# Attention and a squared-ReLU feed-forward on one core: all loads plain on one queue, weights cast on three engines, the whole kernel as one scheduled list

## The chip, the cores and the metric

One core of one Trainium2 chip. The metric is device time in microseconds (us), the median of several executions. The engines are PE (matmuls), ACT (ScalarE), DVE (VectorE), POOL (GpSimd) and SP, which here only issues DMAs.

## The reference

Causal attention in a window of 64 keys over 8 batches, 8 heads, 576 tokens, head size 64; then a feed-forward over the 4608 tokens: 512 to 2048, squared ReLU, 2048 to 512. All inputs and the output are fp32.

```python
scores = (q @ k.transpose(0, 1, 3, 2)) / sqrt(64)
scores = where((rel >= 0) & (rel < 64), scores, -1e9)      # rel = query - key
x = softmax(scores) @ v                                     # -> 4608 x 512
h = maximum(x @ w_in, 0.0)
out = (h * h) @ w_out
```

## The kernel before

Work goes in chunks of 128 tokens and groups of four chunks (512 tokens, 9 groups). For each chunk: k and q are cast to fp16 and transposed; scores (S), exp on ACT, mask on DVE, values (V) on PE, normalising on DVE, transpose of x (X). For each group: 16 up-projection steps (ReLU on ACT, square on DVE), 16 out-projection steps of four matmuls, four evictions. Groups 0 and 1 do their up-projection chunk by chunk, so that PE has work while data still arrives. Groups 0 to 2 of q and k are loaded as one DMA each, with four tokens in a partition (runs of 1 KB); later groups and all of v come in chunks (runs of 256 B).

The parts that the argument needs (cut):

```python
    def load_w_in(quar):                       # casts fp32 -> fp16 on its way, on POOL's queue
        nc.gpsimd.dma_start(
            out=w_in_q[quar][:],
            in_=moe_w_in[:, quar * FQ:(quar + 1) * FQ].rearrange("(c p) n -> p c n", p=P))

    def behind(w, n):                          # makes the SP queue wait until w has landed
        nc.sync.dma_start(out=gate16[:, n:n + 1], in_=w[0:1, 0, 0:1])

    def load_kq(src, g):                       # one group; pieces end where a batch of 576 tokens ends
        st = kqst.tile([P, H, 4 * D], FP32, name="kq_st", tag="kq_st")
        p = 0
        while p < P:
            b, t0 = divmod(512 * g + 4 * p, 64 * NB)
            n = min(P - p, (64 * NB - t0) // 4)
            nc.sync.dma_start(out=st[p:p + n],
                in_=src[b, :, t0:t0 + 4 * n, :].rearrange("h (t r) d -> t h (r d)", r=4))
            p += n
        return st
    # ...
    load_w_in(2)
    cast_v(3, vst[3])
    behind(w_in_q[1], 0)
    kst[1], qst[1] = load_kq(k, 1), load_kq(q, 1)
    # ...
    for g in range(2, NTB + 1):                # the steady part: steps sorted by a place in the group
        # ...
        if g + 2 < NTB:
            steps += [(0.03 + 0.17 * j, load_chunk, 4 * g + 8 + j) for j in range(4)]
            if g + 2 >= KQ_XBAR:
                steps.append((0.8, transposes_xbar, g + 2))    # k and q transposed by DMA
        run(steps)
```

Group 0 fills all 128 partitions from one batch. Group 1 straddles two batches, so its load is two pieces, of 16 and 112 partitions; group 2's has 32 and 96.

The softmax here doesn't subtract the row's maximum and nothing guards it: scores larger than these inputs give would overflow.

## Time and profile before

| | before |
|---|---|
| median time | 330.55 us (329.89 to 330.83; the first three runs) |
| profiled span | 328.0 us |
| third q group (q2) landed | 65.50 us |
| first full-width up-projection (u2.0, group 2) | 90.76 us |
| last matmul | 323.86 us |

Landing times, and the rates in GB/s further down, are counted from the trace's semaphore and packet records. Rates are of bytes read; the page's own GB/s row counts bytes moved to the destination, so a casting load shows half of what it reads.

The page of the kernel before. A digit is the busy share of a fortieth of the span, in tenths; PEclk is the granted clock of PE.

```profile
span 328.0 us, 7256 instructions
...
PE 306.0 (93%) x2896; PEld 162.2 (49%) x2896; DVE 189.7 (58%) x431; ACT 158.7 (48%) x273; POOL 109.6 (33%) x181
...
PE   7758899989899999999999999999999999999994
...
PEclk9999999999999999999999999999999999999998
DMA  7999999989693969598949995799589022000111
```

PE is full from a quarter of the span on, and loose before. DMA is full where PE is loose.

What PE waited for, longest first (total us, times, longest), kernel before:

```profile
PE sc L223 <- DMA qT<-q: 3.7, 5, 0.8
PE hps L298 <- DVE xT L265: 3.7, 3, 2.1
PE run_ps L193 <- DVE k L120: 1.4, 4, 0.5
PE run_ps L193 <- ACT q L120: 1.4, 2, 1.1
```

The first line is in the steady part: five groups start their scores 0.75 us before the DMA transpose of q has ended. Busy time by stretches shows it as PE's missing 0.77 us (start:end length, PE, PEld, DVE, ACT, POOL, clock, DMA share, GB/s):

```profile
120.00:140.00 20.00, 19.23 (x165) 8.96 (x165) 12.17 (x26) 10.62 (x19) 6.21 (x10) 1.00 0.91 177
140.00:160.00 20.00, 19.22 (x146) 9.06 (x147) 10.75 (x24) 9.46 (x17) 6.05 (x10) 1.00 0.92 206
```

In the first part, the timeline of POOL shows casts of k and q that begin as their loads land. The bracket is the idle time before, and what ended it:

```profile
28.62 1.17 POOL L120 CAST k<-kq_st 128x512 f16<-128x512 f32 x2 [7.86 <-DMA kq_st<-in_k_dram]
...
33.62 1.17 POOL L120 CAST q<-kq_st 128x512 f16<-128x512 f32 x2 [3.14 <-DMA kq_st<-in_q_dram]
...
61.17 1.17 POOL L120 CAST k<-kq_st 128x512 f16<-128x512 f32 x2 [15.01 <-DMA kq_st<-in_k_dram]
65.64 1.17 POOL L120 CAST q<-kq_st 128x512 f16<-128x512 f32 x2 [3.31 <-DMA kq_st<-in_q_dram]
```

### The profile page before, as it was taken

To read this page: it belongs to the slowest core of one execution; us is meant where nothing else is said; L and a number is where in the kernel's file an instruction comes from. 1 tells how busy PE (TensorE), PEld (TensorE's weight loads), DVE (VectorE), ACT (ScalarE), POOL (GpSimd) and SP (SyncE) were. 2 spreads that over 40 slices of the span, in tenths; PEclk is the share of its full clock that TensorE was granted. 3 is DMA by queue.
4 is the path that set the end of the run, shared out by engine and by line. 5 is a ranking of instruction groups with operands and counts; after the bars stand their busy time and mean duration, and the time that the engine had idled before them with its cause. 6 is when DMAs were issued, how large, how long until landed. Compare 5 with 4: busy or idle time off the path is not lost.

```text
span 328.0 us, 7256 instructions
## 1 busy us (share of the span) xinstructions
PE 306.0 (93%) x2896; PEld 162.2 (49%) x2896; DVE 189.7 (58%) x431; ACT 158.7 (48%) x273; POOL 109.6 (33%) x181
## 2 busy tenths in 40 slices
PE   7758899989899999999999999999999999999994
PEld 3347668874445444444444444444444444444442
DVE  3776888677656656654656466646654675334400
ACT  3634665485246545544554365445644563444411
POOL 1742850199834522433345243614360000000000
PEclk9999999999999999999999999999999999999998
DMA  7999999989693969598949995799589022000111
GB/s 239 211 179 244 161 165 202 206 188 202 154 219 87 225 140 234 109 215 176 229 114 199 192 228 119 169 224 225 115 165 204 34 66 60 36 34 32 64 64 65
DMA packets 136741, 50.79 MB, mean 155 GB/s; under 512 B 121860, under 2 KB 132100, under 8 KB 136708
## 3 DMA queue, kind: packets, MB, share of 16 engines
q1 hardware_dynamic: 132484, 46.15, 65.6%
q0 software_dynamic: 4224, 4.19, 8.2%
q8 instruction: 22, 0.36, 0.5%
q14 instruction: 11, 0.09, 0.1%
HBM read 36.70 MB, written 9.44 MB: 141 GB/s over the span
## 4 chain that ended last, share of the span: by engine, by line
PE 60%; DMA 13%; DVE 10%; SPq 6%; ACT 5%; issue 3%; POOL 2%; ACTq 0%; POOLq 0%
PE ops L315 28%; PE hps L286 20%; DMA qT<-q 7%; PE hps L298 5%; PE sc L223 3%; SPq L201 3%; ACT hrelu L279 3%; DVE h L280 3%; PE av L247 3%; DMA kq_st<-in_q_dram 2%; DMA st<-in_v_dram 2%; DVE x_sb L252 2%; SPq L84 2%; DVE pm L236 2%; DMA st<-in_q_dram 1%
## 5 line engine op out<-in xcount | busy, mean ns | idle before, releaser
L280 DVE SCALAR_TENSOR_TENSOR h<-hps,hrelu 128x512 f16<-128x512 f32 x144 | 99.3, 690 | 102.4 <-ACT hrelu L279 101.4
L315 PE MATMUL ops<-w_out,h 128*128 128x512 f16 x576 | 145.3, 380 | 0.0
L279 ACT ACTIVATE hrelu<-hps 128x512 f32<-128x512 f32 x144 | 86.1, 598 | 102.7 <-PE hps L286 81.7
L286 PE MATMUL hps<-xT,w_in 128*128 128x512 f16 x448 | 115.1, 379 | 0.0
L315 PEld LDWEIGHTS <-h 128*128 128x128 f16 x576 | 53.7, 98 | 60.9
L286 PEld LDWEIGHTS <-w_in 128*128 128x128 f16 x448 | 42.8, 98 | 50.2
L232 ACT ACTIVATE pm<-sc 128x512 f16<-128x512 f32 x72 | 39.0, 596 | 22.0 <-PE sc L223 21.4
L114 POOL CAST k<-st 128x512 f16<-128x512 f32 x24 | 14.8, 615 | 74.2 <-DMA st<-in_k_dram 73.4
L298 PE MATMUL hps<-xT,w_in 128*128 128x128 f16 x512 | 32.2, 219 | 4.6 <-DVE xT L265 3.7
L321 ACT ACTIVATE osb<-ops 128x512 f32<-128x512 f32 x36 | 21.5, 598 | 28.5 <-PE ops L315 28.5
L298 PEld LDWEIGHTS <-w_in 128*128 128x128 f16 x512 | 29.6, 98 | 6.5 <-issue 5.6
L252 DVE TENSOR_TENSOR x_sb<-av,rden 128x256 f16<-128x256 f32 x72 | 30.6, 425 | 2.5
L236 DVE TENSOR_TENSOR pm<-pm,mask_inner 128x512 f16<-128x512 f16 x56 | 26.9, 505 | 4.1 <-ACT pm L232 3.5
L126 POOL CAST v_ev<-st 128x512 f16<-128x512 f32 x36 | 23.2, 644 | 10.7 <-DMA st<-in_v_dram 8.0
L127 POOL COPY v_od<-v_ev 64x512 f16<-64x512 f16 x36 | 22.4, 623 | 2.3
L129 POOL COPY v_od<-v_ev 64x512 f16<-64x512 f16 x35 | 22.2, 633 | 2.0
L247 PEld LDWEIGHTS <-pm 128*64 128x64 f16 x576 | 12.3, 110 | 14.2 <-issue 11.4
L114 POOL CAST q<-st 128x512 f16<-128x512 f32 x24 | 15.6, 651 | 8.9 <-DMA st<-in_q_dram 8.9
L247 PE MATMUL av<-v_od,pm 128*64 128x65 f16 x288 | 16.3, 197 | 0.5 <-DVE pm L236 0.5
L247 PE MATMUL av<-v_ev,pm 128*64 128x65 f16 x288 | 16.3, 197 | 0.0
L223 PE MATMUL sc<-qT,kT 64*128 64x64 f16 x504 | 15.0, 191 | 1.4 <-DVE x_sb L252 1.1
L223 PEld LDWEIGHTS <-kT 64*128 64x128 f16 x504 | 10.7, 95 | 4.9 <-issue 1.9
(57 smaller groups left out, 121.2 us busy)
## 6 DMA issues: line engine op xcount, KB each, us to landing
out_dram<-osb SPq DMA_DIRECT2D x36, 256.0 KB, 2.6
st<-in_v_dram SPq DMA_DIRECT2D x32, 256.0 KB, 5.3
st<-in_k_dram SPq DMA_DIRECT2D x21, 256.0 KB, 4.1
st<-in_q_dram SPq DMA_DIRECT2D x21, 256.0 KB, 5.1
w_in<-in_moe_w_in_dram POOLq DMA_DIRECT2D x4, 512.0 KB, 6.3
w_out<-in_moe_w_out_dram POOLq DMA_DIRECT2D x4, 512.0 KB, 8.6
kq_st<-in_k_dram SPq DMA_DIRECT2D x1, 1024.0 KB
kq_st<-in_q_dram SPq DMA_DIRECT2D x1, 1024.0 KB, 8.1
```

The source lines that it names most:

```text
L114: copy(out=kq16(key, i // 4)[:, :, i % 4, :].rearrange("p a (b d) -> p a b d", d=D), in_=st[:].rearrange("p (a b) d -> p a b d", b=2))
L126: nc.gpsimd.tensor_copy(out=v_ev[:, :, 0:D], in_=st[:])
L223: nc.tensor.matmul(sc[hh][:, hp, blk, :], keys, qTs["q", g][r0:r0 + 64, hp, a + 64 * blk:a + 64 * blk + 64], start=True, stop=True)
L232: nc.scalar.activation(out=pm[:], in_=sc[hh][:], func=AF.Exp, scale=1.0 / float(D) ** 0.5)
L236: nc.vector.tensor_tensor(out=pm[:], in0=pm[:], in1=mask, op=ALU.min)
L247: nc.tensor.matmul(av[64 * blk:64 * blk + 64, h % 4, 0:65], pms[i][h % 2][:, h // 2, blk, :], vv[:, h, 0:65], start=True, stop=True)
L252: nc.vector.tensor_tensor(out=x_sb[:, 2 * half:2 * half + 2, i % 2, :].rearrange("p c (b d) -> p c b d", d=D), in0=av[:, :, 0:D].rearrange ...
L279: nc.scalar.activation(out=hrelu, in_=hps, func=AF.Relu, scale=H_SCALE)
L280: nc.vector.scalar_tensor_tensor(out=out, in0=hps, scalar=0.0, in1=hrelu, op0=ALU.max, op1=ALU.mult)
L286: nc.tensor.matmul(hps[:], w_in_q[f // 4][:, c, f % 4 * P:(f % 4 + 1) * P], xT_of(g)[:, :, c, :], start=(c == 0), stop=(c == DMC - 1))
L298: nc.tensor.matmul(hps[:, f, :], w_in_q[fq][:, c, f * P:(f + 1) * P], xT_of(g)[:, i % 4 // 2, c, a:a + P], start=(c == 0), stop=(c == DMC ...
L315: nc.tensor.matmul(hold[ts % 2][:], h2s["h", g][:, 4 * fq + f, ts * P:(ts + 1) * P], w_out_q[fq][:, f, :], start=(fq == 0 and f == 0), sto ...
```

## The change

The intent: no engine's program is written by hand any more. Each step (a load, a cast, four matmuls, an eviction) is a word in a list; list scheduling has put the words in order, and each engine executes its own words in that order. All loads go plainly through SP's queue. The weights land as fp32 in the staging buffers that q and k use too (2 buffers became 4), and ACT, DVE and POOL cast them, half a quarter at a time. The gates (`behind`) and 18 of 32 warm-up matmuls are gone.

```diff
+PROGRAM = """
+    lk0 lq0 dv0 ck0.0@A ck0.1@D ck0.2@P dv1 ck0.3@D W14 Tk0.0 Tk0.1 tk0.0@A li0 tk0.1@D cq0.0@A
+    ... (loads: lk lq dv li lo; casts ck cq cv ci co; T S V X U O on PE; @A @D @P: the engine)
+    cq2.0@A cq2.1@D cq2.2@P dv10 cq2.3@D Tk2.0 Tk2.1 tk2.0@A Tq2.0 tk2.1@D dv11 Tq2.1 tq2.0@A
+    O0.2.3 tq2.1@D cv8@P dk12 O0.3.3 Z0.2 cs8@P B2@D U4.0@u cv9@A cn8@P z0.2 Z0.3 U4.1@u cs9@P
+    ...
+"""
-    kqst = ctx.enter_context(tc.tile_pool(name="kqst", bufs=2))
+    kqst = ctx.enter_context(tc.tile_pool(name="kqst", bufs=4))
-    def load_w_in(quar):
-        nc.gpsimd.dma_start(
-            out=w_in_q[quar][:],
-            in_=moe_w_in[:, quar * FQ:(quar + 1) * FQ].rearrange("(c p) n -> p c n", p=P))
+    def load_w_in(n):
+        t = st["i", n] = kqst.tile([P, DMC, FQ], FP32, name="w_st", tag="kq_st")
+        nc.sync.dma_start(
+            out=t[:], in_=moe_w_in[:, n * FQ:(n + 1) * FQ].rearrange("(c p) n -> p c n", p=P))
+    def cast_w(key, n, half, e):
+        w = (w_in_q if key == "i" else w_out_q)[n]
+        copier(e)(out=w[:, 2 * half:2 * half + 2, :], in_=st[key, n][:, 2 * half:2 * half + 2, :])
-    warm(14)
-    cast_run("k", 0, kst[0], 0, acopy)
-    ... (the whole hand-made order, and the sorted steps of the steady part)
+    steps(PROGRAM)
```

## The prediction

> **What bounds it now.** The page gives a 328.0 us span, 330.55 us timed. From 90 us on (busy time by stretches, chain of waits) PE is full: from the first out-projection of group 1 at 90.06 us to the last matmul at 323.9 us, 233.8 us pass, 3.7 of them waiting. The waits view names five waits, 0.75 us each, of the scores for the DMA transpose of q. A steady group takes 31.87 us, of which 32 steps of four 512-column matmuls at 0.866 us are 27.7. This part can shrink only by those waits.
>
> The first 90 us are loose. By my sum (0.866 us per output step, 0.91 per chunk step, 0.85 per attention chunk, transposes) PE does about 62 us of useful work there; the rest is idle (14 us), warm-up matmuls (32) and latency. DMA paces it: its row stands full from 9 to 74 us. The second pair of q and k group loads lands at 33.5 us, the third at 65.5 us. Packets counted by 2 us windows give 370 GB/s read for the weights, 360 for group 0 of q and k, 250 for group 1, 217 for group 2, 210 for v. There are two holes, at 16-18 and 38-41 us, where POOL issues weight loads late behind its casts.
>
> **What the change does.**
> - Weight DMAs no longer cast. No DMA time is saved: 8.4 MB are read either way, at an estimated 350-370 GB/s. The Trainium skill, "DMA: Bandwidth & Descriptors", section "Issuing engines are not separate DMA queues", says that all issuers share the same 16 DMA engines; the packet records agree (share near 1 whichever queue runs). The holes close: about 4 us.
> - 16 half-weight casts of 128x1024, estimated at 1.0-1.25 us from the 0.6 us casts of 512: 18 us over three engines, in stretches that wait for DMA. Little is critical.
> - Queue order: w_in and half of w_out ahead of k1/q1. Estimated landings: w_in 26 us, q1 40, w_out 46, v7 51, q2 61 (was 65.5). The up-projections of group 0 finish near 37 us instead of past 50; chunks 4-7 run at 43-57.
> - 18 of 32 warm-up matmuls go (4 us of PE, filling waits).
> - The list has U4.0 behind the transposes of group 2, so PE waits for q2: U4.0 starts about 65 us (q2, casts 1.2, transposes 1, two output steps 1.7).
> - From U4.0 to u2.0 my sums are PE 26 us, DVE 26 us (squares 0.69, masks 0.51, normalising 0.60): about 28, so u2.0 near 93 us. PE work after it is about 225 us, without the five waits, since the transposes of a group are now issued long before its scores. Tail 4.1 us, as now.
>
> Sum: 93 + 225 + 4 = 322; less some overlap of output steps, span near 320.5, time near 322.5 us. Half of the gain is the earlier q2, half the five waits.
>
> **Prediction: 322.5 us, 8 in 10 within 315.5 to 328.5. Faster by over 2%: 0.58; within 2%: 0.38; slower: 0.04.**
>
> **What would show it.** Right: no PE wait of scores for the q transpose; steady group 31.1 us; DMA without holes from 2 to 65 us; q2 landed at 58-64 us; first U of chunk 4 within 5 us of that. Wrong: plain weight loads under 300 GB/s; the stretch from U4.0 to u2.0 over 31 us; new waits in the steady part.
>
> **What would make it wrong.** Slower: the list is fixed per engine, so one late landing (v, or an output store holding the queue) stalls all behind it; PE's clock may fall back in the thinner first 20 us. Faster: weights at 400 GB/s, or DVE less full than my sum.

## The result and the profile after

| | before | after | predicted |
|---|---|---|---|
| median time | 330.25 us (4 runs) | 325.35 us (325.22 to 325.50) | 322.5 (315.5 to 328.5) |
| ratio | 1 | 0.985 [0.9833, 0.9867] | |
| profiled span | 328.0 | 323.5 | 320.5 |
| w_in, last quarter landed | 38.48 | 26.57 | 26 |
| q1 landed | 33.50 | 43.71 | 40 |
| w_out, last quarter landed | 56.31 | 49.84 | 46 |
| q2 landed | 65.50 | 64.80 | 61 |
| chunk 4's first up-projection (U4.0) | 49.4 | 68.2 | 65 |
| group 2's first up-projection (u2.0) | 90.8 | 96.4 | 93 |
| last matmul | 323.86 | 319.72 | |

The time lies in the range; the gain, 1.5%, stayed under the 2% that had been held more likely than not.

The page of the kernel after:

```profile
span 323.5 us, 7251 instructions
...
PE 303.0 (94%) x2878; PEld 162.9 (50%) x2878; DVE 194.4 (60%) x437; ACT 166.1 (51%) x284; POOL 108.2 (33%) x171
...
PE   7489776999999999999999999999999999999995
...
PEclk9769999999999999999999999999999999999999
DMA  7999999999989989999999999991221022001111
```

PE is as loose in the first eighth as before, DMA is full without a hole, and the granted clock drops in the second and third slice. PE's waits in the kernel after:

```profile
PE run_ps L289 <- ACT q L257: 3.9, 3, 2.0
PE run_ps L289 <- ACT k L257: 2.5, 2, 1.7
PE xt_ps L384 <- DVE x_sb L373: 2.2, 5, 0.9
PE hps L405 <- DVE h L435: 2.2, 6, 0.7
```

The waits for the DMA transpose of q are gone. The first two are waits for casts of k and q, and those casts start when the loads land, as the timeline of ACT shows:

```profile
39.26 1.14 ACT L257 CAST k<-kq_st 128x512 f16<-128x512 f32 x2 [2.70 <-DMA kq_st<-in_k_dram]
...
43.79 1.14 ACT L257 CAST q<-kq_st 128x512 f16<-128x512 f32 x2 [2.00 <-DMA kq_st<-in_q_dram]
...
60.85 1.14 ACT L257 CAST k<-kq_st 128x512 f16<-128x512 f32 x2 [5.50 <-DMA kq_st<-in_k_dram]
64.90 0.62 ACT L257 CAST q<-kq_st 128x512 f16<-128x512 f32 x1 [2.91 <-DMA kq_st<-in_q_dram]
```

By the times in PE's timeline, these waits belong to the groups as follows: 0.82 us for k0 and 2.04 for q0 at the start, 1.65 for k1 (at 39.93 us), 1.66 for q1 (44.46), and only 0.23 for q2 (65.58). So PE waits for group 1; when q2 lands, PE has only just got there.

Busy time by stretches: the steady part is full, and the start is cold (clock 0.59).

```profile
10.00:20.00 10.00, 6.96 (x127) 5.64 (x128) 8.49 (x21) 6.76 (x13) 7.18 (x10) 0.59 1.13 325
120.00:140.00 20.00, 20.00 (x193) 9.60 (x192) 12.35 (x29) 11.22 (x21) 7.81 (x13) 1.00 1.12 207
140.00:160.00 20.00, 20.00 (x150) 9.28 (x149) 11.36 (x24) 9.35 (x17) 8.61 (x15) 1.00 1.24 226
```

**Where the 4.5 us of span come from.** A steady group takes 31.03 us (128.64 to 159.67) where it took 31.87. Take the waits out of before: from 90.06 us it needs 233.8 - 3.7 = 230.1 us to its last matmul. After needs 223.3 us from u2.0 at 96.4, so it stands where before would have stood at 90.06 + 6.8 = 96.9 us. So the start gained only about 0.5 us, the five waits 3.7, the end 0.4 (3.78 us instead of 4.14 from the last matmul to the end). The prediction had wanted some 4 us from the start. Why it gave nearly nothing is what the experiments ask.

### The profile page after: what moved, and what is told of

Read it like the earlier page. It is cut to its first block, busy times and chain, and to the rows that moved or that the text cites. A ratio compares the mean times of both kernels' runs of the same rounds, so it can differ in the third digit from the quotient of the medians.

```text
span 323.5 us, 7251 instructions
## 1 busy us (share of the span) xinstructions
PE 303.0 (94%) x2878; PEld 162.9 (50%) x2878; DVE 194.4 (60%) x437; ACT 166.1 (51%) x284; POOL 108.2 (33%) x171
## 4 chain that ended last, share of the span: by engine, by line
PE 73%; DMA 11%; SPq 6%; DVE 6%; ACT 2%; issue 0%; POOL 0%; ACTq 0%; DVEq 0%
PE ops L449 34%; PE hps L414 30%; SPq L172 6%; DMA w_st<-in_moe_w_out_dram 4%; DMA st<-in_v_dram 4%; PE av L362 3%; PE sc L338 3%; DMA kq_st<-in_q_dram 3%; PE hps L405 2%; DVE pm L354 2%; DVE h L435 1%; DVE x_sb L373 1%; ACT pm L347 1%; SPq L251 1%; PE qkT_ps L303 0%
## 5 line engine op out<-in xcount | busy, mean ns | idle before, releaser
L414 PEld LDWEIGHTS <-w_in 128*128 128x128 f16 x448 | 42.8, 98 | 50.2 <-issue 0.2
L405 PEld LDWEIGHTS <-w_in 128*128 128x128 f16 x512 | 30.6, 100 | 4.1 <-issue 2.1
L274 POOL CAST v_ev<-st 128x512 f16<-128x512 f32 x28 | 17.9, 639 | 40.1 <-DMA st<-in_v_dram 34.8
L354 DVE TENSOR_TENSOR pm<-pm,mask_inner 128x512 f16<-128x512 f16 x56 | 30.0, 565 | 0.7 <-ACT pm L347 0.5
L263 POOL CAST q<-st 128x512 f16<-128x512 f32 x24 | 14.8, 617 | 20.4 <-DMA st<-in_q_dram 19.5
L362 PEld LDWEIGHTS <-pm 128*64 128x64 f16 x576 | 13.0, 113 | 14.1 <-issue 9.4
L362 PE MATMUL av<-v_od,pm 128*64 128x65 f16 x288 | 17.2, 201 | 1.6 <-DVE x_sb L373 1.3
L362 PE MATMUL av<-v_ev,pm 128*64 128x65 f16 x288 | 17.3, 202 | 0.0
L372 DVE RECIPROCAL rden<-av 128x4 f32<-128x4 f32 x72 | 12.5, 174 | 7.8 <-PE av L362 7.5
```

What stands on the lines that cost most here:

```text
L263: copier(e)(out=kq16(key, i // 4)[:, :, i % 4, :].rearrange("p a (b d) -> p a b d", d=D), in_=st[key, i][:].rearrange("p (a b) d -> p a b ...
L354: nc.vector.tensor_tensor(out=pms[i, hh][:], in0=pms[i, hh][:], in1=mask, op=ALU.min)
L362: nc.tensor.matmul(av[64 * blk:64 * blk + 64, h % 4, 0:65], pms[i, h % 2][:, h // 2, blk, :], vv[:, h, 0:65], start=True, stop=True)
L405: nc.tensor.matmul(hps[:, f, :], w_in_q[fq][:, c, f * P:(f + 1) * P], xT_of(i // 4)[:, i % 4 // 2, c, a:a + P], start=(c == 0), stop=(c == ...
L414: nc.tensor.matmul(hps[:], w_in_q[f // 4][:, c, f % 4 * P:(f % 4 + 1) * P], xT_of(g)[:, :, c, :], start=(c == 0), stop=(c == DMC - 1))
```

## The experiments

Theory A, first stated: the landings of q1 and q2 pace the first 97 us. The loads of groups 1 and 2 of q and k ran at only about 200 GB/s, where group 0 ran at 350 to 370, because 112 or 96 partitions divide badly over 16 DMA engines. Rivals: they are slow because engines compute meanwhile (B); landings do not pace, the cold clock or the order does (C). After the first runs came theory D, that the single queue itself costs time, against E, that the gain of the casting DMAs is in the cast. The kernel after has times 325.2 to 325.5 us in all its runs. The table is the whole series but e2, which changes the old kernel; it is read through the text below. All results were correct.

| run | time, us | ratio to before, 95% | q1 | q2 | U4.0 | u2.0 | last matmul | last - u2.0 |
|---|---|---|---|---|---|---|---|---|
| after | 325.35 | 0.985 [0.983, 0.987] | 43.7 | 64.8 | 68.2 | 96.4 | 319.7 | 223.3 |
| e1 | 327.47 | 0.992 [0.989, 0.994] | 45.5 | 67.6 | 71.0 | 99.3 | 322.6 | 223.3 |
| e3 | 325.68 | 0.986 [0.984, 0.988] | 43.2 | 64.3 | 67.7 | 96.1 | 319.6 | 223.5 |
| e4 | 319.79 | 0.968 [0.967, 0.970] | 35.2 | 58.6 | 62.3 | 90.5 | 313.9 | 223.3 |
| e5 | 327.47 | 0.990 [0.986, 0.995] | 47.4 | 67.0 | 71.1 | 99.0 | 322.3 | 223.3 |
| e6 | 328.35 (1 run) | | 46.6 | 67.4 | 70.8 | 99.2 | 322.8 | 223.6 |
| e7 | 319.28 | 0.967 [0.962, 0.973] | 33.6 | 57.7 | 61.6 | 89.2 | 312.9 | 223.7 |
| e8 | 329.55 | 0.999 [0.997, 1.000] | 51.0 | 66.5 | 71.8 | 100.2 | 323.7 | 223.5 |
| e9 | 332.15 | 1.008 [1.004, 1.012] | 37.3 | 63.5 | 73.9 | 102.8 | 326.2 | 223.4 |
| e10 | 322.77 | 0.978 [0.977, 0.980] | 25.1 | 59.2 | 66.1 | 93.6 | 317.0 | 223.4 |
| e11 | 323.58 | 0.980 [0.976, 0.984] | 41.9 | 60.3 | 65.1 | 93.8 | 317.4 | 223.7 |
| e12 | 321.00 | 0.972 [0.967, 0.976] | 41.9 | 55.8 | 62.5 | 90.6 | 313.9 | 223.3 |

The last column is the strongest result: from u2.0 on, every kernel of this list takes 223.3 to 223.7 us. All differences between them arise before u2.0.

### e1: power-of-two pieces

```diff
-            n = min(P - p, (64 * NB - t0) // 4)
+            n = 1 << (min(P - p, (64 * NB - t0) // 4).bit_length() - 1)
```

> The kernel after, with the q and k group loads of groups 1 and 2 cut into pieces of 64, 32 and 16 partitions in place of 112+16 and 96+32 (same bytes, same order). Theory A: the arrivals of q1 and q2 pace the first 97 us, and those loads ran at about 200 GB/s because 112 or 96 partitions divide badly over 16 engines; then they run at 300 GB/s or more, q1 lands 3 to 4 us earlier than 43.7, q2 6 to 8 us earlier than 64.8, and the whole is 4 to 7 us faster than the kernel after (about 319 to 321 us). Rival B: they are slow because compute runs beside them, or because a group straddles two batches: same rates, same 325.4 us within 0.7. Rival C: arrivals do not pace: rates rise, and the time stays at 325.4.

Measured: 327.47 us, q1 at 45.5 and q2 at 67.6. The theory about the division of 112 and 96 fell: pieces of 64 partitions went slower still (512 KB from 34.55 to 38.07 us and from 40.57 to 43.74 us, 149 and 165 GB/s). But time moved with the landings: q1 1.8 and q2 2.75 us later, the last matmul 2.9 us later. The Trainium skill, "SBUF — State Buffer", section "Door 1: The DMA port swizzle", puts partitions 0 to 63 on 8 of the 16 ports that DMA has into SBUF, with 196 GB/s measured there. That is not the case here: the pieces of 64 lie at partitions 16 to 79 (group 1) and 32 to 95 (group 2), which by its table reach 12 and all 16 ports, and in windows of 2 us the pieces of k1 read 148 to 206 GB/s (32 to 40 us). Why they were this slow is not shown; e6 has pieces that do fit the table.

### e2: the five waits alone, in the kernel before

```diff
-                steps.append((0.8, transposes_xbar, g + 2))
+                steps.append((0.65, transposes_xbar, g + 2))
```

> The kernel before, with one change: the DMA transposes of q and k of a group are issued at 0.65 of the group before it and not at 0.8. Theory A: the five waits of the scores for the transpose of q (0.75 us each) are pure loss on PE, so the time falls by 3 to 3.7 us, ratio about 0.99: that is most of what the change to the kernel after gains (4.9 us). Rival: PE is bound by something else there and the time goes elsewhere; under 1 us.

Measured: 327.51 us (325.78 to 328.83), ratio 0.992 [0.987, 0.997], 2.7 us. PE's waits no longer contain the transpose of q; they begin:

```profile
PE hps L298 <- DVE xT L265: 3.7, 3, 2.1
PE run_ps L193 <- DVE k L120: 1.8, 4, 0.6
PE run_ps L193 <- ACT q L120: 1.5, 2, 1.2
```

The profiled span fell by 2.7 us too, its last matmul from 323.86 to 321.11. Behind the first full-width up-projection the trace needs 229.5 us in place of 233.1, 3.6 us less, which is the five waits; that step itself came 0.8 us later (q2 landed at 66.45), before anything that the edit touches. By its mean this one number in the old kernel is worth more than half of the 4.9 us that the rewrite gained. The runs scatter, so the size is 1.2 to 4.3 us.

### e3: warm-up matmuls put back

Fillers W3, W2, W2, W3, W2, W1 in the list between the first transposes and the first up-projection, as before had them.

> The kernel after with the warm-up matmuls of the kernel before put back between Tk0 and the first U (13 more, as before had). Theory A: the granted clock in 10 to 30 us rises from 0.59 and 0.90 to 1.0, chunk 0 to 3's up-projections run faster, but k1 and q1 land when they did, so from 45 us on nothing moves: within 0.7 us of the kernel after. Rival C (the cold clock costs): the whole gets 1 to 3 us faster.

Measured: 325.68 us, no change. The clock came back:

```profile
10.00:20.00 10.00, 8.04 (x158) 5.11 (x158) 8.64 (x22) 6.70 (x13) 5.90 (x9) 1.00 1.12 330
```

In the kernel after, the 16 matmuls of the first up-projection took 1.87 us; before, 1.05. The Trainium skill, "TensorE: Matmul & The Clock Gate", "Part 1: The HAM clock gate", gives half clock after an idle window of about 3.4 us. The trace has the half (the granted clock is 0.5 from 11.82 to 22.06 us), but PE was not idle in the 3.4 us before it: it was busy for 1.12 of 3.42 us (8.40 to 11.82). The cost is real and lands in a stretch where PE will wait for k1 and q1 anyway, so it is worth nothing. Rival C's cold clock is out.

### e4: casting weight DMAs on POOL's queue again, in the new list

```diff
     def load_w_in(n):
-        t = st["i", n] = kqst.tile([P, DMC, FQ], FP32, name="w_st", tag="kq_st")
-        nc.sync.dma_start(
-            out=t[:], in_=moe_w_in[...])
+        nc.gpsimd.dma_start(
+            out=w_in_q[n][:], in_=moe_w_in[...])
     # w_out likewise; the casts ci and co do nothing; the list keeps its order
```

> The kernel after with the weights loaded by casting DMAs from POOL as in the kernel before, no staging and no casts on the engines; all else in the list stays. Theory A: both kinds of weight load read at 370 to 385 GB/s, and the engine casts sit in waits, so the time stays within 2 us of 325.4; q2 lands within 2 us of 64.8. If the plain loads are what the kernel after gains by, it is 4 us or more slower.

Measured: 319.79 us, 5.6 us faster than the kernel after. This was a clear miss of theory A, and the most useful run. So half of the change works against the other: the list with the old kind of weight load gains 10.4 us, and the plain loads on the one queue give back 5.6.

The weights did not read faster: 375 to 388 GB/s in the kernel after (20 to 28 us), 371 to 378 in before (18 to 22 us). Behind q2 the engine casts were not what cost: u2.0 came 31.6 us behind q2 in the kernel after and 32.0 in e4. What moved are the landings: q1 8.5 us earlier, q2 6.2. In e4 the loads of k1, q1 and v4 to v7 were issued by SP from 10 to 38 us beside the weights. From 24 to 32 us, in windows of 2 us, both queues together read 341 to 367 GB/s: 107 of k and q, 245 of weights on average. Where k and q have the machine to themselves, they read 187 to 223 (after, 32 to 40 us). As an estimate from these packets: the 0.86 MB of q and k and 1.96 MB of weights of those 8 us would have taken 4.1 us at 210 and 5.2 us at 380 GB/s one after the other, 9.3 us.

That saves 1.3 us, and q2 came 6.2 us earlier. The same count over the whole start, from the landing of the first chunk of v (10.6 us) to that of q2, tells the rest. Its third column is an estimate: all bytes that were read or stored there, one kind after the other, at 380 GB/s for weights and stores of the output, 210 for k and q, 205 for v (the rates of the kernel after where each moves alone).

| | 10.6 us to q2 | the same bytes one kind after the other | difference |
|---|---|---|---|
| before | 54.8 us | 52.1 us | 2.7 lost |
| after | 54.1 us | 51.4 us | 2.7 lost |
| e4 | 47.9 us | 51.3 us | 3.4 saved |
| e8 (below) | 55.8 us | 51.9 us | 3.9 lost |

So of the 6.2 us about 3.4 are overlap, and about 2.7 are time that the one queue lost and e4 did not, most of it where weights and smaller loads take turns (0.6 us from 28 to 32, 1.7 from 40 to 50 us). With 220 GB/s for k and q the parts are 2.5 and 3.6.

PE's waits in e4, and the cast of q2 on ACT's timeline (64.90 in the kernel after). The waits for q and k in this list are those of group 0, at 10.05 and 6.97 us:

```profile
PE hps L403 <- DMA w_in<-in_moe_w_in_dram: 2.9, 2, 1.6
PE run_ps L287 <- ACT q L256: 2.0, 1, 2.0
...
PE run_ps L287 <- ACT k L256: 1.0, 1, 1.0
```

```profile
58.66 0.62 ACT L256 CAST q<-kq_st 128x512 f16<-128x512 f32 x1 [2.93 <-DMA kq_st<-in_q_dram]
```

For q1 and q2 PE did not wait at all. From 18 us to U4.0 it stood idle for 7.9 us in the kernel after and 3.8 in e4: gone are 3.3 us for k1 and q1, 1.1 for casts of w_out and 2.0 for x (which comes out of attention on group 1), new are 2.9 for w_in. So the late loads cost time through group 1; that U4.0 comes 3.4 to 4.1 us behind q2 in most runs is for the most part not a wait for q2 (0.2 to 1.2 us in after, e1, e3 and e6, none in e4, e5 and e7).

### e5: plain weight loads, but from POOL's queue

```diff
-        nc.sync.dma_start(
+        nc.gpsimd.dma_start(
             out=t[:], in_=moe_w_in[...])       # and w_out
```

> The kernel after with one change: the eight plain weight loads are issued from POOL's queue and not from the SP queue; staging, casts and list stay. The run with casting DMAs from POOL came out 5.6 us faster than the kernel after, against Theory A; in its packets weights and small loads moved together at 340 to 365 GB/s, where the one queue moves 1 KB and 256 B loads alone at about 200. Theory D: the gain is the second queue, not the cast: q2 lands at 58 to 61 us, the time is 319 to 322 us. Rival E: it is the cast (half the bytes written to SBUF, no staging, no casts on the engines): q2 lands at 63 us or later, the time is within 1.5 us of 325.4.

Measured: 327.47 us, q2 at 67.0. Against theory D as written, but it does not speak for E either: the two queues hardly overlapped. Weight loads stood in POOL's program behind casts that wait for earlier loads, and shared four staging buffers with q and k; DMA read 33 GB/s from 22 to 24 us, and k1 moved alone from 36 to 44 us. Inconclusive.

### e6: group 0 cut up, as a control

```diff
             n = min(P - p, (64 * NB - t0) // 4)
+            if g == 0:
+                n = min(n, 112 if src is k else 64)
```

> Control for the rate of the group loads: in the kernel after the load of k0 is cut into 112+16 partitions and that of q0 into 64+64, all at the start, when no engine computes. If fewer than 128 partitions make a load slow, k0 and q0 take 4 to 5 us each and q0 lands at 11.5 us or later in place of 9.5. If the loads of groups 1 and 2 are slow because other engines compute meanwhile, q0 lands within 0.5 us of 9.5.

Measured (one run): k0 landed at 8.26 and q0 at 13.27 us, where the kernel after has 6.41 and 9.51 (q0: 9.35 to 9.75 in all other runs). No engine computed at that time but for warm-ups and k0's own casts and transposes. The timeline of ACT, e6:

```profile
8.34 0.62 ACT L259 CAST k<-kq_st 128x512 f16<-128x512 f32 x1 [6.04 <-DMA kq_st<-in_k_dram]
...
13.35 0.62 ACT L259 CAST q<-kq_st 128x512 f16<-128x512 f32 x1 [2.53 <-DMA kq_st<-in_q_dram]
```

So partial width alone makes such loads slow (171 to 253 GB/s from 4 to 12 us instead of 350 to 370), and computing beside them is not needed for it. By the table of "SBUF — State Buffer" each half of q0 (partitions 0 to 63 and 64 to 127) reaches 8 ports, and 213 and 206 GB/s from landing to landing are near the page's 196. For 112 the ports are not the reason: by the same table, partitions 0 to 111 reach all 16, and they were slow as well.

### e7: e4 with five copies moved from DVE to ACT

```diff
-    x8@D ... x9@D ... x10@D ... x11@D ... cv10@D
+    x8@A ... x9@A ... x10@A ... x11@A ... cv10@A
```

> The kernel with casting weight DMAs (319.8 us) with five copies of the stretch from chunk 4's first up-projection to group 2's first (x8 to x11 and the cast of v10) moved from DVE to ACT. That stretch takes 28.2 us in every run, with DVE 97% busy for its middle 10 us and PE waiting 1 to 2 us in all. If DVE limits it, the stretch is 1 to 2.4 us shorter and the time 317.5 to 319; if PE does, no change within 0.6.

Measured: 319.28 us, not to be told from e4. U4.0 to u2.0 went from 28.2 to 27.6 us, DVE's busy time in it from 24.1 to 22.8, PE's stayed at 26.4 and 26.3. So PE is the nearer limit of this stretch; DVE adds half a microsecond.

### e8: e4 with the overlap taken away

```diff
-    ... R3.1 lk1 Q0.2 ...
+    ... R3.1 g3 lk1 Q0.2 ...        # g3: a tiny DMA on SP that reads the last quarter of w_out
+                                    # (and lo2 lo3 moved up behind lo1)
```

> The kernel with casting weight DMAs (e4, 319.8 us), but the load of k1 waits until the last quarter of w_out has landed (a tiny DMA that reads it stands ahead of k1 on the SP queue), so that weights and small loads follow one another as in the kernel after. Theory D (overlap of two queues is what e4 gained): q2 lands at 63 to 66 us again, the stretches after it keep their lengths, and the time is 324 to 327 us. Rival E (it was the cast: fewer bytes written, no casts on the engines): q2 stays below 61 us, the time within 2 us of 319.8.

Measured: 329.55 us, q1 at 51.0, q2 at 66.5: 9.8 us slower than e4 with the same casting loads. E as it was stated is out. But the time does not measure the overlap, since the gate makes PE wait for k1 by itself:

```profile
PE run_ps L292 <- ACT k L261: 9.9, 1, 9.9
```

The landings tell more, though DMA had two holes: one that the gate makes (199 GB/s from 36 to 38 us, 2 from 38 to 40), and one at 24 to 26 us (52 GB/s), behind the last quarter of w_in, which k1 and q1 fill in e4. By the count under e4 they cost an estimated 4.7 us. Without them q2 would have landed near 61.8 us, about halfway between e4 (58.6) and the kernel after (64.8). So theory D holds for about half of what q2 gained in e4.

### e9: plain loads from POOL's queue, staging split in two and two

Weights have two buffers of their own, k and q two; each weight load stands in the list right behind the casts that free its buffer.

> The other half of the test: plain weight loads from POOL's queue with engine casts, staged in two buffers of their own, each load issued right behind the casts that free its buffer; k1 and q1 have their own two buffers and are issued at 10 to 20 us as in e4 (e5 failed to overlap: its loads stood behind POOL's waits for casts, with a hole at 22 us and k1 alone at 36 to 44 us). Theory D: q1 lands at 34 to 40 us, q2 at 58 to 62, the time 319 to 323 us. Rival E: q2 at 64 or later, 325 or more.

Measured: 332.15 us. q1 landed early, at 37.3, but two weight buffers made w_out late (its first use on PE was at 49.99 us; 37.25 in the kernel after) and k2 had to wait for a buffer and was issued at 50 us. PE's largest wait was for squares (3.4 us, until 44.12). DVE stood idle before them, waiting for ACT's ReLU, and ACT's order had a cast of w_out ahead of that ReLU, which waited for its load:

```profile
PE hps L406 <- DVE h L436: 5.6, 5, 3.4
```

```profile
41.80 1.04 ACT L271 CAST w_out<-w_st 128x1024 f16<-128x1024 f32 x1 [4.03 <-DMA w_st<-in_moe_w_out_dram]
```

So a weight cast in an engine's fixed order can hold up the work behind it. The test of the queue apart from the cast failed again, through scarcity of staging. The trace shows only that plain loads overlap too: from 26 to 32 us both queues together read 333 to 349 GB/s, but k and q had only 67 to 74 of it, and by the count under e4 this saved 0.2 us of 6.2. It stays open whether plain loads on a second queue with ample staging would do as well as casting ones; what is shown is that casting loads from POOL's queue, which need no staging and no engine casts, are together worth 5.6 us here.

### e10: e7 with q1 and q2 on ACT's queue

```diff
-        st[key + "g", g] = load_kq(SRCS[key], g)
+        st[key + "g", g] = load_kq(SRCS[key], g, nc.scalar if key == "q" and g > 0 else None)
     # list: lq1 behind cv1@A, lk1 behind dv3, lk2 behind dv7, lq2 behind E6.0
```

> Towards a better version: e7 (319.3 us) with the loads of q1 and q2 on ACT's queue, beside k1 and k2 on SP. If two partial-width loads side by side move faster than one after the other (together over 220 GB/s), q2 lands at 53 to 56 us and the time is 315.5 to 318.5. If 1 KB loads of fewer than 128 partitions are limited together, q2 lands at 57 to 59 us, no change within 1 us; if the weights are held back by two rival queues, PE waits for w_in and it gets slower.

Measured: 322.77 us, slower than e7. q1 came at 25.1 us, far ahead of need, and the second quarter of w_in at 26.4 instead of 21.1 in e4:

```profile
PE hps L404 <- DMA w_in<-in_moe_w_in_dram: 5.1, 1, 5.1
```

More queues are not better by themselves: what lands next must be what is needed next. (From 16 to 18 us only ACT's queue moved anything, 159 GB/s; the records do not say why.) Whether two partial-width loads are faster side by side stays open: k2 and q2 overlapped for under 2 us.

### e11: full-width pieces for groups 1 and 2

384 tokens of one batch, three to a partition on all 128 partitions (768 B runs); the other 128 tokens, one to a partition. The copies that follow the transposes put the tokens in order.

```diff
+    FULL = {1: [(0, 64, 0, 512, 0), (0, P, 1, 0, None), (64, P, 1, 384, 448)],
+            2: [(0, P, 1, 448, 0), (0, P, 2, 0, None)]}
     def load_kq(src, g):
+        if g in FULL:
+            for (p0, p1, b, t0, o) in FULL[g]:
+                if o is None:
+                    nc.sync.dma_start(out=st[:, :, D:4 * D],
+                        in_=src[b, :, t0:t0 + 3 * P, :].rearrange("h (t r) d -> t h (r d)", r=3))
+                else:
+                    nc.sync.dma_start(out=st[p0:p1, :, 0:D],
+                        in_=src[b, :, t0:t0 + p1 - p0, :].rearrange("h p d -> p h d"))
+            return st
```

> The kernel after, with the loads of groups 1 and 2 laid out so that their large piece has 128 partitions: 384 tokens, three to a partition (768 B runs), and the other 128 tokens one to a partition (256 B); the copies after the transposes put the tokens back in order. Same bytes, one queue. e6 showed that pieces under 128 partitions move at 170 to 250 GB/s even at the quiet start, against 350 to 370 at full width. Expected: the large piece at 280 GB/s or more, k1+q1 and k2+q2 about 2 us shorter each, q1 at 41 to 42 us, q2 at 60 to 62 (64.8), and the whole earlier by as much: 321 to 323.5 us against 325.4. If q2's landing does not set the time, q2 moves and the time doesn't; if runs of 768 and 256 B are as slow as the partial width, neither moves.

Measured: 323.58 us (322.44 to 326.38). q1 at 41.9 and q2 at 60.3, as expected; the last matmul 2.3 us earlier. The way there was the expected one for group 2 alone: from v7 to q2 7.6 us instead of 10.1. For group 1, k1 and q1 took 9.4 us instead of 9.7, and what came earlier was the quarter of w_out ahead of them (32.51 instead of 34.02). The large pieces, expected at 280 GB/s or more, read 231 and 283 (group 1) and 248 and 339 (group 2) from landing to landing. By the ratios 0.985 and 0.980 it is 1.8 us faster than the kernel after; the intervals just touch. So of 4.5 us in q2 only half reached the end: U4.0 now came 4.8 us behind q2 instead of 3.4, since other work of PE stood before it (PE did not wait for q2).

### e12: the same in e7

> The same layout in e7 (casting weight DMAs on POOL's queue, five copies moved to ACT; 319.3 us): the fastest version of what the runs point to. If q2 (57.7 there) still sets the time, 1 to 3 us faster: 316.5 to 318.5. If PE is full by then (it waits 1.5 us in all between 60 and 92), under 1 us.

Measured: 321.00 us (319.29 to 322.42), no faster than e7 although q2 landed at 55.8 us, 2 us earlier. U4.0 is at 62.5 us, 6.7 us behind q2. Here q2 has stopped setting the time. In PE's waits the longest is again for q (2.1 us for q0, 1.7 for q1):

```profile
PE run_ps L303 <- ACT q L272: 3.8, 2, 2.1
```

A likely cause, not tested, is at group 1: q1 came in at 41.9 us, against 33.6 in e7, its last piece behind two queues' worth of traffic.

The version that beats both kernels is e4: 319.79 us, ratio 0.968 [0.967, 0.970]; e7 is its equal.

## Why the prediction was right or wrong

- **The time (322.5 predicted, 325.35 measured)** lies in the range. The class that had 0.58, faster by over 2%, did not come; the gain is 1.5%.
- **The five waits: right.** They are gone from PE's waits, a steady group takes 31.03 us (31.1 predicted), and e2 gives the same step alone 2.7 us [1.2, 4.3] in the old kernel, 3.6 of it behind u2.0 in its trace.
- **The sum behind q2: right.** q2 to U4.0 3.4 us (4 predicted), U4.0 to u2.0 28.2 (28), u2.0 to the last matmul 223.3 (225), tail 3.8 (4.1). That "PE waits for q2" was barely so: it waited 0.23 us for it, and 3.3 us for k1 and q1, so part of this match is luck.
- **The landing of q2: the mis-sized term.** "Estimated landings: w_in 26 us, q1 40, w_out 46, v7 51, q2 61": the first was right (26.57), q1 came at 43.71, and the 3.7 us between stayed to the end (49.84, 54.71, 64.80). Two parts make it. The second quarter of w_out landed at 34.02, where q1 at 40 less 8.4 us for 2.1 MB at the prediction's 250 GB/s has it at 31.6; in its last 2 us (30 to 32) its 2 KB packets took 259 ns instead of 88 and all of DMA read 127 GB/s, as the 112-partition piece of k1 began. Then k1 and q1, 2.1 MB, took from 34.02 to 43.71, 216 GB/s instead of 250. Partial width keeps such pieces under 350 to 370 (e6; e11 for group 2). But the same pieces had read 233 to 278 in the kernel before (24 to 30 us) and 187 to 223 here (32 to 40 us): why is not shown, and why the hand-over is so slow was not tested either.
- **"Weight DMAs no longer cast. No DMA time is saved ... The holes close: about 4 us": half right, and it hid the loss.** The rates are equal and the holes did close, 3.4 us by the count under e4. But on the same count the kernel before had saved about 2 us from 22 to 38 us, with two queues at work, and the kernel after loses 2.7 us, most of it where weights and small loads take turns in the one queue. So q2 gained only 0.7 us; the estimate had priced neither. e4 against the kernel after shows 5.6 us for staged plain loads on one queue against casting loads on a second one, and e8's landings put about half of what q2 gained there on the overlap. How much the engine casts and the staging have in the rest was not taken apart. I had leaned on the Trainium skill, "DMA: Bandwidth & Descriptors", section "Issuing engines are not separate DMA queues", which says that several issuers save only the sequencer's time. For this mix of loads the packets say otherwise: what one after the other would take an estimated 51.3 us took 47.9 in e4.
- **"Half of the gain is the earlier q2": wrong in result.** q2 came 0.7 us earlier, and the start gained about 0.5 us.
- **The casts cost little: right behind q2** (u2.0 31.6 us behind it with them, 32.0 without); ahead of it PE waited 1.1 us for casts of w_out. **The clock may fall back: right, and harmless** (e3).

## What to carry to other kernels

Before a kernel's loads are put in one queue, sum them per kind at the rate that each kind reaches alone; if a kind leaves bandwidth unused (few partitions, short runs), keep it beside the long loads on a second queue (shown here with casting loads; plain ones did not gain in e5 and e9), and check that the order of landing is still the order of need. When a rewrite changes many things at once, put each one back alone: here one half of it gained 10.4 us and the other gave back 5.6, and a single constant in the old kernel was worth 2.7. And find the moment from which all variants take equally long (here 223.3 to 223.7 us from u2.0): what matters lies before it.

## What the Trainium skill lacked or had wrong

- "DMA: Bandwidth & Descriptors", "Issuing engines are not separate DMA queues", and its rule that spreading DMAs over issuers does not help bandwidth: for this mix of loads it did. Partial-width 1 KB loads and casting weight loads on two queues read 341 to 367 GB/s together, in 8 us what would have taken an estimated 9.3 us one after the other; over the whole start that saved an estimated 3.4 us (e4). Plain weight loads beside the same loads saved 0.2 us of 6.2 (e9, 26 to 32 us).
- "SBUF — State Buffer", "Door 1: The DMA port swizzle": right for 64 partitions on 8 ports (213 and 206 GB/s in e6), but pieces of 64 that by its table reach 12 ports were slower (149 and 165 GB/s in e1), and pieces of 112 and 96 partitions, which reach all 16, ran at about 200 to 230 GB/s too (e6; k1 and q1 at 216 GB/s), against 350 to 370 for 128. No page gives a rate for a number of partitions between 64 and 128.
- No page tells what a hand-over between loads of different width in one queue costs: 2 KB packets went from 88 to 259 ns, and DMA read 127 GB/s for 2 us (kernel after, 30 to 32 us).
